# Last tokens of k and v in head halves, two v loads as bf16, and a new order of loads and of chunk 0's side work, in an attention and MLP kernel

## The chip, the core and the metric

The kernel runs on one core of one Trainium2 chip. The metric is the device time of one execution in microseconds; lower is better.

## The reference

```python
# q, k, v: (8 batches, 8 heads, 576 tokens, 64), fp32
q_s = exp(q - max(q)); q_s = q_s / sum(q_s, axis=-1)      # softmax over the head dimension
k_s = exp(k - max(k)); k_s = k_s / sum(k_s, axis=2)       # softmax over the tokens
kv  = einsum('bhsd,bhse->bhde', k_s, v)                   # one 64 x 64 matrix per head
x   = einsum('bhsd,bhde->bhse', q_s, kv)                  # then heads side by side: (8, 576, 512)
xn  = (x - mean(x)) / sqrt(var(x) + 1e-6) * g_ln
out = x + relu(xn @ w_ch1) @ w_ch2                        # w_ch1 512 x 2048, w_ch2 2048 x 512
```

## The kernel before

**Tiles and chunks.** A batch has 576 tokens: 512 main ones, token `4p + t` on partition `p` with `t` from 0 to 3, and 64 last ones. The program is a sequence of nine chunks of 512 tokens: chunks 0 to 7 are the main tokens of the batches, chunk 8 (`C9`) the last tokens of all eight batches together. For the keys, batch 0 has a layout of its own, 96 partitions of six tokens; in the others the key-value product of a pair of heads `j` (`kv_mm`, L239 to 263) takes four matmuls over the main tokens (`ek` as weights, `vm` as the moving operand, with a column of ones that gives the sum of k) and a fifth over the last tokens (`ekr`, `vr`). The last tokens of batch `b` lie on partitions 0 to 63 or 64 to 127, by the parity of `b`; the other half of `ekr` and `vr` is zero.

**A chunk.** The main stream of a chunk (`mlp_steps`) is its two MLP products: `mm1` (L406, 128x512 matmuls into `ph`, whose relu to `hT` is ACT's) or `mm1_part` (L421, the same on one or two of the four `t`), and then `mm2_stream` (L466) in chunk 0 and a seven-product scheme (L513, `ba` to `be`, with sums on DVE, L497) in the others. A chunk can start once its `xnT` is there: `x` from `po_mm` (L283) and `x_fast` (L329), normalized to `xn` on DVE, and transposed, either by the DMA (`xn_T`, on SP's queue) or by TensorE and a copy out of PSUM (`pe_T`, L788, called by `xn_pT` and `eq_pT`).

**The order** is written out by hand. `run` walks through the main stream, adds up a weight for every matmul (1 for 512 columns, 0.5 for 256), and emits each side step once the sum has reached the step's position. In chunk 0 positions run from 0 to 128. Each engine then works its instructions off in that order. Side steps of chunk 0 are the rest of batch 0's attention and all of batch 1's: exp of q, transposes of `eq`, exp of k, `cast_v` (L147, fp32 `vt` into bf16 `vm`, DVE), `prep_kvrem` (L155), `kv_all(1)` at 96, `po_x(1, t)` from 96.5 to 106, the transposes of `xn` at 104 to 126, and at 127 exp of q for batch 2. Chunk 1 holds batch 2's attention (`second_side`), chunk 2 batch 3's (`attn_fast`), and so on.

**Before chunk 0** stands `first_batch` (L812): batch 0's q (two of four `t`), k, exp, transposes, kv and po for `t` 0 and 1, with matmuls on zeros (`warm`) between them. Its DMAs: q and k on SP's queue, all others on POOL's, in this order: v (two blocks), w1 block 0, the other half of q, w1 blocks 1 to 3, w2 blocks 0 and 1. `load_behind(1)` (L911) then adds batch 1's q, k, v and last tokens, `load_w2` the last two blocks of w2, `load_behind(2)` batch 2's. A load on POOL's queue that writes another type than it reads is a cast in flight: the weights and batch 0's v come so. POOL's DMAs go round over eight semaphores, so that an issue waits for the landing of the one eight before it. Batches 3 to 7 are loaded on SP's queue, in the chunk two ahead.

The tile `vt` has one buffer, and batch 0's `ek` uses the same one; `kt` has one, `qt` two.

Of the kernel before, what the change touches and what calls it, by code (L numbers as in the profile page):

```python
# [12 lines left out]
FP32 = mybir.dt.float32  # L13
# [7 lines left out]
def kernel(  # L21
# [16 lines left out]
    nc = tc.nc  # L38
# [14 lines left out]
    C9 = B  # L53
    FAST = 1
    T0 = 6
    P0 = S // T0
# [25 lines left out]
    kv_sb = const.tile([P, B, NP, P], BF16)  # L82
    ekr = const.tile([P, 2, H, D], BF16)
    vr = const.tile([P, 2, NP, VW], BF16)
# [4 lines left out]

    def load_w1(nb):  # L90
        cols = slice(nb * 512, nb * 512 + 512)
        nc.gpsimd.dma_start(w1_sb[:, :, cols], w1_src[:, :, cols])
# [10 lines left out]
    def alloc_batch(b):  # L103
        raws[b] = (
            raw.tile([P, H, T, D], FP32, tag="kt", name="kt", bufs=1),
            raw.tile([P, H, T, D], FP32, tag="vt", name="vt", bufs=1),
            raw.tile([P, H, T, D], FP32, tag="qt", name="qt"),
            raw.tile([P, H, D], FP32, tag="ktr", name="ktr"),
            raw.tile([P, H, D], FP32, tag="vtr", name="vtr"),
        )  # L110
# [8 lines left out]
    def load_kvrem(eng, b):  # L119
        pb = SR * (b % 2)  # L120
        for src, dst in ((k, raws[b][3]), (v, raws[b][4])):
            eng.dma_start(dst[pb : pb + SR], src[b, :, SM:S, :].transpose([1, 0, 2]))

# [31 lines left out]
    def prep_kvrem(b):  # L155
        par = b % 2
        pb = SR * par
        nc.scalar.activation(ekr[pb : pb + SR, par], raws[b][3][pb : pb + SR], AF.Exp)
        nc.vector.tensor_copy(
            out=vr[pb : pb + SR, par, :, 0:P],  # L160
            in_=raws[b][4][pb : pb + SR].rearrange("p (j h) d -> p j (h d)", h=2),
        )

# [75 lines left out]
    def kv_mm(b, j, t):  # L239
        par = b % 2  # L240
        last = T if b else T0 - 1
        if j % 2 == 0 and t == 0:
            kvbox["p"] = att_ps.tile([P, 2, 256], FP32, tag="a", name="pkv")
        pkv = kvbox["p"]
        w = P + 1
        if b == 0:
            lhsT, rhs, w = k0_mm(j, t)
        elif t < T:
            lhsT, rhs = eks[b][:, t, 2 * j : 2 * j + 2, :], vm[:, par, t, j, 0 : P + 1]
        else:  # L250
            lhsT, rhs = ekr[:, par, 2 * j : 2 * j + 2, :], vr[:, par, j, 0 : P + 1]
        nc.tensor.matmul(  # L252
            pkv[:, j % 2, 0:w], lhsT, rhs, start=(t == 0), stop=(t == last)
        )
        if j % 2 == 1 and t == last:
            js = slice(j - 1, j + 1)
            rzk = recip_z(pkv[:, :, P]) if b else kvbox["rz", j // 2]
            for half in range(2):
                ps = slice(64 * half, 64 * half + 64)
                nc.vector.tensor_mul(  # L260
                    kv_sb[ps, b, js, ps], pkv[ps, :, ps],
                    rzk[ps].to_broadcast([64, 2, D]),
                )
# [51 lines left out]
    def square_sum(c, t):  # L315
        x, _, _, mv = xs[c]
        nc.scalar.activation(  # L317
            scrap, x[:, t], AF.Square, bias=mv[:, t, 0:1], accum_out=mv[:, t, 1:2]
        )
# [27 lines left out]
    def mean_x(c, t):  # L347
        nc.scalar.activation(
            scrap, pobox[c, t], AF.Copy, scale=-1.0 / DM, accum_out=xs[c][3][:, t, 0:1]
        )  # L350
# [289 lines left out]
    def mlp_steps(c):  # L640
        full = range(KO2)
        first, parts = [], ()
        if c == 0:
            full = range(0)
            parts = ((0, 0, 1), (0, 1, 1), (1, 0, 2), (2, 0, 2), (3, 0, 2), (0, 2, 2), (1, 2, 2), (2, 2, 2), (3, 2, 2))
        else:
            full, parts = range(4, KO2), ((0, 0, 2), (0, 2, 2))
        for n, t0, tn in parts:
            first += [
                (0.25 * tn, lambda m=m, t0=t0, tn=tn, ko=ko: mm1_part(c, m, t0, tn, ko))  # L650
                for m in range(4 * n, 4 * n + 4) for ko in range(KO1)
            ]
# [10 lines left out]
    def spread(fns, a, b):  # L663
        n = len(fns)
        return [(a + (b - a) * i / n, fn) for i, fn in enumerate(fns)]
# [63 lines left out]
    def sums_fast(c, t0=0):  # L729

        eq, zq, rq = eqs[c]
        s = spread([lambda t=t: nc.vector.reduce_sum(zq[:, t], eq[:, t], axis=AX.X) for t in range(T)][t0:], 0, 12)  # L732
        return s + [(12, lambda: nc.vector.reciprocal(rq, zq))]

# [14 lines left out]
    def second_side():  # L749

        s = [(p, lambda i=i: quarter_w2(i, 1)) for i, p in enumerate((1, 4, 44, 46))]
        s += [(42, lambda: square_sum(1, 2)), (46, lambda: square_sum(1, 3)), (54, lambda: rstd_op(1))]
        s += [(p, lambda w=w: load_batch(3, (w,))) for p, w in ((8, 2), (31, 0), (40, 1))]
        s += [(p + 11, fn) for p, fn in sums_fast(2)]
        s += [(12, lambda: exp_k(2, 0, 4)), (17, lambda: exp_k(2, 2, 4)), (23, lambda: prep_kvrem(2))]
        s += [
# [3 lines left out]
        s += spread(  # L760
            [lambda j=j, t=t: kv_mm(2, j, t) for j in range(NP) for t in range(T + 1)], 35, 48
        )
        s += [(49, lambda: start_x(2))]
        for t, (p0, p1) in enumerate(((51, 56), (66, 73), (76, 81), (87, 93))):
            s += spread([lambda t=t, i=i: po_mm(2, t, i) for i in range(NP)], p0, p1)
            s += [(p1, lambda t=t: x_fast(2, t)), ((63, 82, 92, 105)[t], lambda t=t: square_sum(2, t))]
        s += [(78, lambda: xn_T(2, 0, 2)), (98, lambda: xn_T(2, 2, 2)), (106, lambda: rstd_op(2))]
# [44 lines left out]
    def first_batch():  # L812
# [44 lines left out]
        nc.gpsimd.tensor_copy(out=gate[0:P0], in_=k0[0:P0, 5, 0, 0:4])  # L857
        load_w1(0)
        load_q0(1, nc.gpsimd)
        for nb in range(1, 4):  # L860
            load_w1(nb)
# [9 lines left out]
        exp_k0(0)  # L871
        nc.vector.memset(vr[:, :, :, P:], 1.0)
        nc.vector.memset(vr[:, :, :, 0:P], 0.0)
        nc.vector.memset(ekr, 0.0)
        nc.vector.memset(vm[:, :, :, :, P:], 1.0)
# [19 lines left out]
        xn, mv = xs[0][2], xs[0][3]  # L895
        stats(0, 0, pobox[0, 0], (slice(0, DH2), slice(DH2, DM)))
        mean_x(0, 1)
        warm(11)
        for i in range(2):
# [10 lines left out]

    def load_behind(b):  # L911

        alloc_batch(b)
        for which in (2, 0, 1):
            load_main(nc.gpsimd, b, which, 0, H)
        load_kvrem(nc.gpsimd, b)

# [11 lines left out]
    with tc.manual_schedule(  # L929
# [3 lines left out]
        first_batch()  # L933
        load_behind(1)
        load_w2(2)
        load_w2(3)
        load_behind(2)
# [5 lines left out]

        def kv_all(c):
            for j in range(NP):
                for t in range(T + 1):
                    kv_mm(c, j, t)
            start_x(c)

        run(  # L950
            mlp_steps(0),
            [
                (0.5, lambda: (xn_pT(0, 1, nc.scalar), exp_qt(0, 2), exp_qt(0, 3))),
                (8, lambda: (eq_pT(0, 2, nc.vector), eq_pT(0, 3, nc.vector))),
                (12, lambda: (q0_rest(2), x_fast(0, 2))),
                (14, lambda: (q0_rest(3), x_fast(0, 3))),
                (24, lambda: xn_pT(0, 2, nc.scalar)),
                (27, lambda: xn_pT(0, 3, nc.vector)),
                (28, lambda: square_sum(0, 2)),
                (32, lambda: square_sum(0, 3)),  # L960
                (34, lambda: (x_copy(0, 0), square_po(0, 1))),
# [5 lines left out]
            + [(67 + t, lambda t=t: reduce_q(1, t)) for t in range(T)]  # L967
            + [((72, 76, 86, 90)[t], lambda t=t: eq_pT(1, t, nc.scalar)) for t in range(T)]
            + [(78, lambda: nc.vector.reciprocal(eqs[1][2], eqs[1][1]))]
            + [(80, lambda: exp_k(1, 0, 4)), (84, lambda: exp_k(1, 2, 4))]  # L970
            + [(94 + 0.2 * j, lambda j=j: cast_v(1, j)) for j in range(NP)]
            + [(p, lambda i=i: quarter_w2(i, 0)) for i, p in enumerate((55, 58, 60, 62))]
            + [(95.9, lambda: prep_kvrem(1))]
            + [(96, lambda: kv_all(1))]
            + [(96.5, lambda: (po_x(1, 0), po_x(1, 1)))]
            + [(100, lambda: po_x(1, 2)), (104, lambda: xn_pT(1, 0, nc.scalar)), (105, lambda: square_sum(1, 0))]
            + [(106, lambda: po_x(1, 3)), (112, lambda: xn_pT(1, 1, nc.scalar)), (113, lambda: square_sum(1, 1))]
            + [(118, lambda: xn_pT(1, 2, nc.scalar))]
            + [(126, lambda: xn_pT(1, 3, nc.scalar)), (127, lambda: (exp_q(2, 0, 4), exp_q(2, 2, 4)))]
            + [(127.8, lambda: eq_T(2))],  # L980
        )
# [53 lines left out]
```

## Time and profile before

| | us |
|---|---|
| median of 5 runs (lowest, highest) | 284.0 (282.36, 285.41) |
| the profiled execution | 284.0 |
| its span (first to last instruction) | 282.2 |
| PE, DVE, ACT busy | 273.3, 196.6, 182.2 |
| first matmul of chunk 0, chunk 1, chunk 2 | 17.2, 54.5, 82.6 |
| HBM read and written | 36.7 MB, 9.4 MB |

A row of the page names line, engine, operation, output and inputs by the program's names, and after the bar busy time, the mean time of one in ns, and the engine's idle time before them with what ended most of it. `PEld` is the load of matmul weights. A line of the chain has start, length, and what the time went to; a line of a timeline has start, length, engine, line, operation, shape, count and, in brackets, the idle time before it and its releaser. A matmul's own length includes its way through the array; in a row of matmuls they start 216 (512 columns), 109 (256) or 56 ns (128) apart.

### The profile page before, as it was taken

The page shows a single profiled execution, that of the slowest core. Times are in us where ns is not written, and L with a number is a line of the kernel's source. Part 1 is how long each engine was busy: PE and PEld are TensorE (multiplying, and loading weights), DVE is VectorE, ACT ScalarE, POOL GpSimd, SP SyncE. Part 2 cuts the span into 40 slices and gives each one's busy share as a digit, 9 for nine tenths or more (in the row PEclk, how much of TensorE's full clock was granted, in tenths as well). Part 3 has the DMA queues.
Part 4 walks back from the last instruction along what each step waited for, and adds up shares of the span by engine and source line. Part 5 has one row for each costly group of instructions (what it writes and reads, how often), then busy time and mean ns, then how long its engine had stood idle before and what let it go on. Part 6 is the DMA issues. An engine that isn't in the chain of part 4 may idle for free.

```text
span 282.2 us, 5607 instructions
## 1 busy us (share of the span) xinstructions
PE 273.3 (97%) x2225; PEld 200.2 (71%) x2228; DVE 196.6 (70%) x452; ACT 182.2 (65%) x344; POOL 34.8 (12%) x61
## 2 busy tenths in 40 slices
PE   8989998999999999999999999999999999999994
PEld 6768855655996588649964986499659855885583
DVE  4655568967997778667866786678667939961363
ACT  4455882698786787597759775977586377526500
POOL 3653213300011002000110020002000200030000
PEclk9999999999999999999999999999999999999999
DMA  7999999999768985995399649953923420142014
GB/s 185 189 231 203 336 241 299 305 236 346 162 133 274 319 84 128 287 306 90 86 288 319 98 111 291 291 97 97 236 42 64 126 77 1 37 114 74 2 37 112
DMA packets 67084, 49.06 MB, mean 174 GB/s; under 512 B 40177, under 2 KB 63217, under 8 KB 67058
## 3 DMA queue, kind: packets, MB, share of 16 engines
q1 hardware_dynamic: 56914, 27.66, 42.4%
q0 software_dynamic: 9552, 20.52, 27.9%
q10 hardware_dynamic: 592, 0.52, 0.5%
q8 instruction: 17, 0.28, 0.4%
q14 instruction: 9, 0.07, 0.1%
HBM read 36.70 MB, written 9.44 MB: 163 GB/s over the span
## 4 chain that ended last, share of the span: by engine, by line
PE 73%; DMA 15%; DVE 7%; ACT 3%; issue 1%; POOL 0%; ACTq 0%; DVEq 0%
PE ph L406 25%; PE ba L513 17%; PE ph L421 9%; DMA vt<-in_v_dram 8%; DMA qt<-in_q_dram 4%; PE bb L513 4%; PE bc L513 4%; PE be L513 4%; PE pkv L252 2%; DMA v<-in_v_dram 2%; PE pc L466 2%; PE po L283 2%; ACT hT L394 2%; DVE hs L497 2%; DVE ot L524 1%
## 5 line engine op out<-in xcount | busy, mean ns | idle before, releaser
L406 PE MATMUL ph<-xnT,w_sb 128*128 128x512 bf16 x384 | 90.6, 379 | 0.0
L394 ACT ACTIVATE hT<-ph 128x512 bf16<-128x512 f32 x96 | 55.4, 597 | 17.4 <-PE ph L406 17.4
L406 PEld LDWEIGHTS <-w_sb 128*128 128x128 bf16 x384 | 35.6, 98 | 36.6
L513 PEld LDWEIGHTS <-hs 128*128 128x128 bf16 x512 | 49.1, 98 | 5.8 <-DVE hs L497 0.2
L421 PE MATMUL ph<-xnT,w_sb 128*128 128x256 bf16 (+1 forms) x400 | 49.3, 268 | 1.2 <-DMA w_sb<-in_moe_w_ch_dram 1.1
L431 ACT ACTIVATE hT<-ph 128x512 bf16<-128x512 f32 x44 | 25.8, 596 | 26.6 <-PE ph L421 26.6
L497 DVE TENSOR_TENSOR hs<-hT 128x1024 bf16<-128x1024 bf16 x32 | 21.9, 687 | 29.5 <-ACT hT L394 29.3
L513 PEld LDWEIGHTS <-hT 128*128 128x128 bf16 x384 | 36.6, 98 | 6.0 <-ACT hT L394 0.9
L421 PEld LDWEIGHTS <-w_sb 128*128 128x128 bf16 x400 | 35.1, 98 | 5.5 <-DMA w_sb<-in_moe_w_ch_dram 1.8
L530 POOL DMA_DIRECT2D out_dram<-ot x28 | 15.0, 540 | 182.6 <-DVE ot L524 182.6
L513 PE MATMUL ba<-w_q,hs 128*128 128x256 bf16 x256 | 31.3, 273 | 0.0
L323 DVE SCALAR_TENSOR_TENSOR xn<-x,mv,g_bc 128x512 bf16<-128x512 bf16 x34 | 25.5, 751 | 1.2
L330 DVE SCALAR_TENSOR_TENSOR x<-po,rq 128x512 bf16<-128x512 f32 x30 | 20.6, 685 | 7.1 <-PE po L283 6.8
L317 ACT ACTIVATE scrap<-x,mv 128x512 bf16<-128x512 bf16 x34 | 24.5, 720 | 0.4 <-DVE mv L336 0.2
L283 PE MATMUL po<-kv_sb,eqT 128*128 128x128 bf16 x128 | 24.0, 219 | 0.5 <-DVE kv_sb L260 0.5
L252 PE MATMUL pkv<-vm,ek 128*128 128x129 bf16 x112 | 21.8, 220 | 0.0
L538 ACT COPY s<-ba 128x512 f32<-128x512 f32 x15 | 8.8, 586 | 15.9 <-PE ba L513 15.6
L283 PEld LDWEIGHTS <-eqT 128*128 128x128 bf16 x128 | 11.5, 98 | 7.7 <-issue 0.9
L513 PE MATMUL ba<-w_sb,hT 128*128 128x256 bf16 x128 | 16.4, 273 | 0.5 <-ACT hT L394 0.5
L732 DVE TENSOR_REDUCE zq<-eq 128x8 f32<-128x512 bf16 x26 | 16.3, 692 | 0.1
L176 ACT ACTIVATE eq<-qt 128x1024 bf16<-128x1024 f32 x14 | 14.5, 1054 | 2.1 <-DMA qt<-in_q_dram 2.1
L513 PE MATMUL bb<-w_q,hs 128*128 128x256 bf16 x128 | 15.7, 273 | 0.0
(121 smaller groups left out, 343.6 us busy)
## 6 DMA issues: line engine op xcount, KB each, us to landing
out_dram<-ot POOLq DMA_DIRECT2D x32, 256.0 KB, 2.9
qt<-in_q_dram SPq DMA_DIRECT2D x5, 1024.0 KB, 7.0
kt<-in_k_dram SPq DMA_DIRECT2D x5, 1024.0 KB, 9.8
vt<-in_v_dram SPq DMA_DIRECT2D x5, 1024.0 KB, 12.6
w_sb<-in_moe_w_ch_dram POOLq DMA_DIRECT2D x8, 512.0 KB, 14.1
qt<-in_q_dram POOLq DMA_DIRECT2D x2, 1024.0 KB, 19.0
kt<-in_k_dram POOLq DMA_DIRECT2D x2, 1024.0 KB, 16.5
vt<-in_v_dram POOLq DMA_DIRECT2D x2, 1024.0 KB, 18.0
```

The costliest lines, as they stand in the source:

```text
L252: nc.tensor.matmul(pkv[:, j % 2, 0:w], lhsT, rhs, start=(t == 0), stop=(t == last))
L283: nc.tensor.matmul(pobox["p"][:, i * P : i * P + P], eqTs[c][:, t, i, :], kv_sb[:, c, i, :], start=True, stop=True,)
L317: nc.scalar.activation(scrap, x[:, t], AF.Square, bias=mv[:, t, 0:1], accum_out=mv[:, t, 1:2])
L323: nc.vector.scalar_tensor_tensor(xn[:, t], in0=x[:, t], scalar=mv[:, t, 0:1], in1=g_bc, op0=ALU.add, op1=ALU.mult)
L330: nc.vector.scalar_tensor_tensor(x[:, t].rearrange("p (h d) -> p h d", h=H), in0=pobox[c, t].rearrange("p (h d) -> p h d", h=H), scalar=1. ...
L394: nc.scalar.activation(dst, src, AF.Relu)
L406: nc.tensor.matmul(hbox["ph"], w1_sb[:, ko, m * P : (m + 1) * P], xnTs[c][:, :, ko, :], start=(ko == 0), stop=(ko == KO1 - 1),)
L421: nc.tensor.matmul(ph[:, m % 2, at : at + tn], w1_sb[:, ko, m * P : (m + 1) * P], xnTs[c][:, t0 : t0 + tn, ko, :], start=(ko == 0), stop=( ...
L431: nc.scalar.activation(dst, ph, AF.Relu)
L497: nc.vector.tensor_tensor(out=dst, in0=x, in1=y, op=op)
L513: nc.tensor.matmul(hbox[bank][:, t], lhsT, rhs, start=first and (own or t == 0) and k == 0, stop=k == KH - 1, skip_group_check=True)
L732: s = spread([lambda t=t: nc.vector.reduce_sum(zq[:, t], eq[:, t], axis=AX.X) for t in range(T)][t0:], 0, 12)
```

## The change

- The last tokens of k and v go by halves of the heads: heads 0 to 3 on partitions 0 to 63, heads 4 to 7 on 64 to 127, for every batch. Two DMAs become four, `ekr` is half as wide, exp works on 128 x 256 instead of 64 x 512, the copy into `vr` becomes two of 64 x 256. The number and shape of kv matmuls stay.
- `vt` of batches 1 and 2 is bf16; their loads, on POOL's queue, cast in flight, and `cast_v` copies bf16.
- POOL's queue: the other half of batch 0's q comes ahead of w1 block 0, which comes in two halves of 256 columns; w2 block 2 comes ahead of batch 1's v.
- `first_batch` takes exp of that q half and the transposes of `eq` for `t` = 2 in among its own work; two `warm` matmuls fewer.
- Chunk 0: the quarter `(3, 0, 2)` of its first product goes later; the rest of batch 0's attention moves earlier, batch 1's from `cast_v` on later; the kv products of the last tokens stand 1.5 positions behind the others (and use both PSUM tiles). Exp and transposes of q for batch 2, and the fourth transpose of `xn` for batch 1, move into chunk 1.
- Chunk 1: two blocks of its first product instead of one are done by halves of `t`, both first halves first; batch 2's attention is placed later in it.

```diff
+    CAST = (1, 2)
...
-    ekr = const.tile([P, 2, H, D], BF16)
+    ekr = const.tile([P, 2, H // 2, D], BF16)
...
+    def load_w1(nb, c0=0, c1=512):
+        cols = slice(nb * 512 + c0, nb * 512 + c1)
...
-            raw.tile([P, H, T, D], FP32, tag="vt", name="vt", bufs=1),
+            raw.tile([P, H, T, D], BF16 if b in CAST else FP32, tag="vt", name="vt", bufs=1),
...
     def load_kvrem(eng, b):
-        pb = SR * (b % 2)
         for src, dst in ((k, raws[b][3]), (v, raws[b][4])):
-            eng.dma_start(dst[pb : pb + SR], src[b, :, SM:S, :].transpose([1, 0, 2]))
+            for half in range(2):
+                eng.dma_start(
+                    dst[SR * half : SR * half + SR],
+                    src[b, 4 * half : 4 * half + 4, SM:S, :].transpose([1, 0, 2]),
+                )
...
     def prep_kvrem(b):
...
+        nc.scalar.activation(ekr[:, par], raws[b][3], AF.Exp)
+        for half in range(2):
+            ps = slice(SR * half, SR * half + SR)
+            nc.vector.tensor_copy(
+                out=vr[ps, par, 2 * half : 2 * half + 2, 0:P],
+                in_=raws[b][4][ps].rearrange("p (j h) d -> p j (h d)", h=2),
+            )
...
-            parts = ((0, 0, 1), (0, 1, 1), (1, 0, 2), (2, 0, 2), (3, 0, 2), (0, 2, 2), (1, 2, 2), (2, 2, 2), (3, 2, 2))
+            parts = ((0, 0, 1), (0, 1, 1), (1, 0, 2), (2, 0, 2), (0, 2, 2), (1, 2, 2), (2, 2, 2), (3, 0, 2), (3, 2, 2))
...
+            if c == 1:
+                full, parts = range(8, KO2), ((0, 0, 2), (1, 0, 2), (0, 2, 2), (1, 2, 2))
...
     def second_side():
...
+        s += [(8.0, lambda: xn_pT(1, 3, nc.scalar))]
+        s += [(10, lambda: exp_q(2, 0, 4)), (14, lambda: exp_q(2, 2, 4)), (14.2, lambda: eq_T(2))]
...
-            [lambda j=j, t=t: kv_mm(2, j, t) for j in range(NP) for t in range(T + 1)], 35, 48
-        )
-        s += [(49, lambda: start_x(2))]
-        for t, (p0, p1) in enumerate(((51, 56), (66, 73), (76, 81), (87, 93))):
+            [lambda j=j, t=t: kv_mm(2, j, t) for j in range(NP) for t in range(T + 1)], 43, 53
+        )
+        s += [(53, lambda: start_x(2))]
+        for t, (p0, p1) in enumerate(((55, 58), (64, 67), (75, 80), (87, 93))):
...
-        load_w1(0)
         load_q0(1, nc.gpsimd)
+        load_w1(0, 0, 256)
+        load_w1(0, 256, 512)
...
+        exp_qt(0, 2)
         mean_x(0, 1)
-        warm(11)
+        exp_qt(0, 3)
+        warm(6)
+        eq_pT(0, 2, nc.scalar)
+        warm(3)
...
-        load_behind(1)
+        load_behind(1, (2, 0))
         load_w2(2)
+        load_behind(1, (1,))
         load_w2(3)
         load_behind(2)
...
-                (0.5, lambda: (xn_pT(0, 1, nc.scalar), exp_qt(0, 2), exp_qt(0, 3))),
-                (8, lambda: (eq_pT(0, 2, nc.vector), eq_pT(0, 3, nc.vector))),
-                (12, lambda: (q0_rest(2), x_fast(0, 2))),
-                (14, lambda: (q0_rest(3), x_fast(0, 3))),
-                (24, lambda: xn_pT(0, 2, nc.scalar)),
-                (27, lambda: xn_pT(0, 3, nc.vector)),
+                (0.5, lambda: xn_pT(0, 1, nc.scalar)),
+                (1.5, lambda: (q0_rest(2), x_fast(0, 2))),
+                (3, lambda: eq_pT(0, 3, nc.scalar)),
+                (6, lambda: (q0_rest(3), x_fast(0, 3))),
+                (9, lambda: xn_pT(0, 2, nc.scalar)),
+                (15, lambda: xn_pT(0, 3, nc.scalar)),
...
-            + [(94 + 0.2 * j, lambda j=j: cast_v(1, j)) for j in range(NP)]
+            + [(98.5 + 0.2 * j, lambda j=j: cast_v(1, j)) for j in range(NP)]
...
-            + [(95.9, lambda: prep_kvrem(1))]
-            + [(96, lambda: kv_all(1))]
-            + [(96.5, lambda: (po_x(1, 0), po_x(1, 1)))]
-            + [(100, lambda: po_x(1, 2)), (104, lambda: xn_pT(1, 0, nc.scalar)), (105, lambda: square_sum(1, 0))]
-            + [(106, lambda: po_x(1, 3)), (112, lambda: xn_pT(1, 1, nc.scalar)), (113, lambda: square_sum(1, 1))]
-            + [(118, lambda: xn_pT(1, 2, nc.scalar))]
-            + [(126, lambda: xn_pT(1, 3, nc.scalar)), (127, lambda: (exp_q(2, 0, 4), exp_q(2, 2, 4)))]
-            + [(127.8, lambda: eq_T(2))],
+            + [(100.4, lambda: prep_kvrem(1))]
+            + [(100.5, lambda: kv_main(1)), (102.0, lambda: kv_rest(1))]
+            + [(108.0, lambda: po_x(1, 0)), (110.0, lambda: po_x(1, 1))]
+            + [(113.0, lambda: po_x(1, 2)), (114.9, lambda: xn_pT(1, 0, nc.scalar)), (115.9, lambda: square_sum(1, 0))]
+            + [(115.9, lambda: po_x(1, 3)), (121.0, lambda: xn_pT(1, 1, nc.scalar)), (122.0, lambda: square_sum(1, 1))]
+            + [(128.0, lambda: xn_pT(1, 2, nc.scalar))]
```

## The prediction

> **What bounds the kernel now.** I read the page first, then the chain of waits in order of time, then PE's timeline, then the DMA issues one by one.
>
> ```profile
> PE 273.3 (97%) x2225; PEld 200.2 (71%) x2228; DVE 196.6 (70%) x452; ACT 182.2 (65%) x344; POOL 34.8 (12%) x61
> ...
> DMA  7999999999768985995399649953923420142014
> ```
>
> TensorE is busy all along, yet the DMA engines (one digit is 7.06 us) are full for the first ten slices. Which of the two sets the end of the opening is told by the chain:
>
> ```profile
> 19.32 22.54 DMA vt<-in_v_dram
> 41.88 1.48 DVE vm L153 x4
> 43.39 0.44 DVE vr L159
> 43.87 0.51 PE pkv L252 x6
> ...
> 54.69 3.49 PE ph L421 x32
> ```
>
> Until 41.9 us the chain is one transfer, batch 1's v (v1 below; k1, q1 alike); then four casts, the copy of its last tokens, the key-value products (kv), and from 54.7 on TensorE to the end. From chunk 3 on each chunk takes 28.1 us, and 32 matmuls of 109 ns, 48 of 216, 112 of 109 and 36 of 56 add to 28.1: nothing is to be had there. Chunk 2 takes 0.6 more, a hole at 99.0 behind ACT's exp of q, whose load (85.6 to 93.7) and place stay; I leave it as it is. So what counts is when the last kv product of batch 1 runs, and how much of TensorE's program is still queued behind it. PE's timeline of the opening has the holes:
>
> ```profile
> 21.10 1.05 PE L421 MATMUL ph<-xnT,w_sb 128*128 128x256 bf16 x8 [0.72 <-DMA w_sb<-in_moe_w_ch_dram]
> ...
> 26.22 0.83 PE L421 MATMUL ph<-xnT,w_sb 128*128 128x256 bf16 x6 [0.38 <-DMA w_sb<-in_moe_w_ch_dram]
> ...
> 43.87 0.22 PE L252 MATMUL pkv<-vr,ekr 128*128 128x129 bf16 x1 [0.45 <-DVE vr L159]
> ...
> 46.08 0.49 PE L283 MATMUL po<-kv_sb,eqT 128*128 128x128 bf16 x6 [0.53 <-DVE kv_sb L260]
> ...
> 54.52 1.69 PE L421 MATMUL ph<-xnT,w_sb 128*128 128x256 bf16 x14
> ```
>
> Counted from start to start against 216, 109 and 56 ns, 2.9 us are lost between 14.95 and 43.03 us (weights late), 1.7 us around kv.
>
> **The queue.** Times from issue to landing of single loads on POOL's queue (KB, us):
>
> ```profile
> kt<-in_k_dram POOLq DMA_DIRECT2D x1, 1024.0 KB, 20.7
> vt<-in_v_dram POOLq DMA_DIRECT2D x1, 1024.0 KB, 22.5
> ktr<-in_k_dram POOLq DMA_DIRECT2D x1, 128.0 KB, 21.1
> vtr<-in_v_dram POOLq DMA_DIRECT2D x1, 128.0 KB, 19.2
> w_sb<-in_moe_w_ch_dram POOLq DMA_DIRECT2D x1, 512.0 KB, 18.6
> ```
>
> Issued at 16.6, 19.3, 21.3, 23.9 and 26.5, they land at 37.3, 41.8, 42.4, 43.1 and 45.0. The whole list: second v of batch 0 13.1, w1 block 0 16.3, q0b (batch 0's other q half) 18.8, w1 blocks 1 to 3 at 21.1, 23.7, 26.2, w2 blocks 0 and 1 at 28.7 and 31.2, q1 34.3, k1 37.3, v1 41.8, and as above. Hence the prices: 2.5 us for a weight block, 3.0 us for 1 MB in fp32, and 45.0 - 37.3 - 3.0 - 2.5 = 2.2 us for k's and v's last tokens together. In plain first-in order v1 would land at 40.3 and vtr at 42.5; they came 1.5 and 0.6 later, since neighbours overlap.
>
> **The change, part by part.**
>
> 1. *w1 block 0 in two halves, behind q0b.* The order leaves the sum alone. The halves make pieces of 512 B where the block had 1 KB: a block's 512 pieces take 2.5 us (4.9 ns each), batch 0's v, 384 pieces of 768 B, 1.42 us (3.7 ns). Between 2.5 us (by bytes) and 3.05 (both pieces' packet times extended) I take 2.8: **+0.3**. q0b lands at 13.1 + 0.76 (the first load's start) + 2.43 = 16.25. TensorE now has the transposes of eq(0,2) between its warm-ups: exp of 0.62 us puts them at 16.9, 1.4 after the first six warm-ups; ACT then works off mean_x, exp_qt(0,3) and a copy before the two xnT copies, so the first ph is at about 18.8 instead of 17.2. Free only under cover of the queue, see 5.
>
> 2. *w2 block 2 ahead of v1.* **+2.5** for v1 and its last tokens; the 0.29 us that PE waited for this block at 45.06 go.
>
> 3. *v1 as bf16.* 1024 pieces of 512 B: the same 2.8 instead of 3.0, **-0.2**. The cast becomes a bf16 copy, which no row shows from SBUF. Ends: 0.35 us from start to start (the fp32 rows, 1.48 for four) and half of it; I take 0.25, so the fourth is done 1.05 us after the first starts. Batch 2's v, which landed at 57.1 and was cast from 60.7, has cover.
>
> 4. *Last tokens by head halves.* Bytes and pieces stay; two DMAs become four, alternating between the partition halves. The Trainium skill (DMA: Bandwidth & Descriptors, Rules for kernel authors) says of two transfers to disjoint partition halves "Don't bother": they serialize on the same 16 engines. By it the 2.2 us stay. The row against it: the eight qr loads of batch 6's stage, 128 KB each and alternating halves, on SP's queue; the third lands at 203.2 and the eighth at 205.6, 0.47 us each, where ktr and vtr on POOL's cost 1.1. Ends 0.9 and 2.2; I take **1.5**. The POOL queue holds eight loads: each issue waits for the landing of the one eight before. v1's waits for w1 block 1 (21.4), the four halves' for later weights (24 to 31.5): all long before their turn. On ACT exp is 256 elements wide (an estimate of 0.41, from 0.63 at 512 and 1.05 at 1024), on DVE two copies of about 0.29 replace 0.42.
>
> Sum: k1 lands at 37.6, w2 block 2 at 40.1, v1 at 42.9 plus a lag of 0.9 (less than before's 1.5, the neighbours being shorter) = 43.8, the last half of vtr at 42.9 + 1.5 + 0.6 = 45.0. Casts end at 44.9, the second vr copy starts then or when its half has landed, after the first copy: 45.5. **Last kv product at 45.55**, against 44.72 before: 0.85 later.
>
> 5. *The new chunk 0 order.* It must let TensorE be there in time. Before, 25.2 us of work lay between 14.95 and 43.03; now five mm2 matmuls more and two warm-ups fewer, 26.1, plus 2.7 of waits from part 1: at the kv products at 43.7, where the first cast is ready at 44.1. Against the last kv product the slack is half a microsecond.
> Behind the kv products chunk 0 has left, by the built order, 26 mm2 matmuls (5.62), 16 po and 12 transposes (1.57) and 0.1 of waits: 7.3, chunk 1 at 52.85. Before there were 32, 16 and 16 and 1.1 of waits: 9.8, at 54.52. So chunk 1 starts **1.65 us earlier**. The price: the fourth xn transpose stands in chunk 1 (0.22), and 64 half-width matmuls there instead of 32 and 16 wide ones (0.04 more). Net -1.4.
>
> 6. *Moved into chunk 1.* xn_pT(1,3) stands at step 8, 16 matmuls after the chunk's first, 55.0; its xn is the fourth of a DVE chain of 1.58 us each from 47.2, so 53.6. exp_q(2) and exp_k(2) stand among relus on ACT (16 of 0.5 us and 4 of 1.05 in 14 us): covered. eq_T(2) now stands behind batch 3's q on SP: issued at about 57.5, it shares the engines with that 1 MB (3.0), batch 2's tail and chunk 0's stores, and lands at 63 to 65.5; po(2,0) at step 55 needs it at 66. Cover about 1 us, and beyond it PE stalls in order. The five SP batches behind have four small loads for two; SP ends them at 95.2 in chunk 2, the transposes behind it wait for xn until 97.0 and are needed at 111.5.
>
> The profiled execution took 284.0 us (span 282.2), which is also the median of the runs shown: 284.0 - 1.4 = **282.6**.
>
> **Rivals.** (a) *The forecast*, 0.50; its own range 281.6 to 283.8.
> (b) *A cast costs by the piece.* Every cast load in the trace has one packet per piece, where fp32 loads pack four; if a 512 B piece costs a w1 piece's 4.9 ns, w1's halves and v1 take 5.0 us each, 2.2 more than I take, and the last kv product is at 49.95: 282.6 + 4.4 = **287.0**. It decides (slower than before) once the queue is over 1.4 us later than forecast. Against it stands batch 0's v, at 3.7. Chance 0.12.
> (c) *The queue is quicker and TensorE binds.* If q0b, whose 128 packets of 4 KB the trace could move in 1.6 us, lands near 15, part 1's waits shrink by 1.2; with last tokens at 0.9 and no lag, kv's end is set by TensorE's arrival, 42.5 + 1.1 = 43.6: **280.7**. Chance 0.22.
> (d) *The change does not do what it says*: halves serialize, 2.2 us, copies stay at 0.35. vtr at 45.7, last kv at 46.3: **283.3**. Chance 0.16.
>
> A rule on the clock bears on (a): the skill (TensorE: Matmul & The Clock Gate, its table for kernels) warns of PE-idle gaps over about 3 us, after which the clock is halved for 3.4 us. Part 1's 1.4 and 1.1 lie apart by 0.9 of work; the holes of before (up to 0.9) left the granted clock at full. By the rule at its worst 1.7 us of work would be lost, of which 0.5 are covered: 283.8, inside the range.
>
> **Numbers.** Range 280.4 to 285.2: below it lies the best of (c), above it most of (b). Over 1% (2.8 us, about what a measurement of this kernel can tell): faster (c) and the edge of (a), 0.27; slower (b) and a late eqT, 0.14; within, 0.59.
>
> **What would show it.** In the profile after: v1 landing at 43 to 44.5; the last pkv<-vr,ekr near 45.5; the first 256-wide ph of chunk 1 near 52.9, no hole of 0.53 for kv_sb; first ph later than before; chunks from 3 on at 28.1. The forecast is wrong if v1 lands after 45.5 or before 42.5, if kv waits neither for vm nor vr, if po(2,0) waits for eqT, or if PEclk drops near 17.

## The result, and the profile after

The changed kernel takes **281.2 us** (median; 280.4 to 283.4) against 283.1 us for the kernel before in runs on the same chip: ratio 0.9929, 95% interval 0.9911 to 0.9948. That is 1.9 us less (1.5 to 2.5 by the interval), where 1.4 us was forecast and 282.6 us predicted. The profiled execution of the changed kernel took 280.9 us (span 279.2).

The page of the changed kernel: busy time of the engines, and the DMA engines' share in 40 slices.

```profile
PE 272.8 (98%) x2239; PEld 201.7 (72%) x2242; DVE 194.9 (70%) x456; ACT 182.0 (65%) x347; POOL 37.7 (14%) x66
...
DMA  6999999999949945994599469944914410141014
```

The sums hardly move. The DMA engines are full for the first eleven slices, as they were for ten before; what changed is which of the two sides the chain of waits follows in the opening (start, length, what):

```profile
12.63 10.86 DMA w_sb<-in_moe_w_ch_dram
23.54 10.65 PE ph L427 x96
...
52.08 1.75 PE ph L427 x16
```

Before, the chain lay on the transfer of v1 until 41.9 us. Now the last transfer on it is w1 block 2, landed at 23.49, and from 23.54 us on it is TensorE, but for DVE's work on kv and x (44.3 to 48.6). So the queue has stopped being the bound around the key-value products (kv), as rival (c) had it. TensorE's timeline there:

```profile
42.91 1.07 PE L257 MATMUL pkv<-vm,ek 128*128 128x129 bf16 x16
...
44.03 0.40 PE L257 MATMUL pkv<-vr,ekr 128*128 128x129 bf16 x4
...
46.02 0.27 PE L289 MATMUL po<-kv_sb,eqT 128*128 128x128 bf16 x2 [0.18 <-DVE kv_sb L266]
...
48.66 0.38 PE L289 MATMUL po<-kv_sb,eqT 128*128 128x128 bf16 x4 [0.19 <-DVE x L336]
...
51.92 1.91 PE L427 MATMUL ph<-xnT,w_sb 128*128 128x256 bf16 x16
```

Neither kv group has a bracket: no wait for `vm` or `vr`. The last kv product starts at 44.03 + 3 x 0.056 = 44.2 us (44.7 before), and chunk 1's first 256-wide `ph` at 51.92 (54.52 before): 2.6 us earlier. The landings behind it, from the DMA issues on POOL's queue (KB, us from issue to landing; w2 block 2 is issued at 18.65, batch 1's v at 21.52, the last of the four halves, of v, at 31.43, w2 block 3 at 34.40):

```profile
w_sb<-in_moe_w_ch_dram POOLq DMA_DIRECT2D x1, 512.0 KB, 20.7
...
vt<-in_v_dram POOLq DMA_DIRECT2D x1, 512.0 KB, 20.8
...
vtr<-in_v_dram POOLq DMA_DIRECT2D x1, 64.0 KB, 11.7
...
w_sb<-in_moe_w_ch_dram POOLq DMA_DIRECT2D x1, 512.0 KB, 11.1
```

v1 lands at 42.27 and all last tokens at 43.13, 0.86 us behind it. All in all, from the landing of the load ahead of v1 to that of the load behind the last tokens (w2 block 2 at 39.31, w2 block 3 at 45.46) 6.15 us pass. In the kernel before the same stretch (k1 at 37.27, w2 block 2 at 45.02) took 7.75. This stretch, called **block to block** below, is the measure used for the queue, because neighbouring loads overlap and single landings mislead. It drifts too: in the three other profiles with these loads in this order (improved, q_first, q0b_behind) it is 5.9 to 6.4 us, and the last tokens land 0.8 to 1.4 us behind v1.

The two profiles differ by 3.0 us of span: chunk 1 starts 2.6 us earlier, and chunk 2's hole of 0.6 us at 99.0 is missing in this execution, against about 0.26 of work moved into chunk 1. The timed medians differ by 1.9 only: before's profiled execution lay 0.9 us above its median of 283.1, after's 0.3 below its own.

### The profile page after: what moved, and what is told of

Its sections match the earlier page's. It is cut to its first block, busy times and chain, and to the rows that moved or that the text cites. A ratio compares the mean times of both kernels' runs of the same rounds, so it can differ in the third digit from the quotient of the medians.

```text
span 279.2 us, 5663 instructions
## 1 busy us (share of the span) xinstructions
PE 272.8 (98%) x2239; PEld 201.7 (72%) x2242; DVE 194.9 (70%) x456; ACT 182.0 (65%) x347; POOL 37.7 (14%) x66
## 4 chain that ended last, share of the span: by engine, by line
PE 89%; DMA 6%; DVE 2%; POOL 1%; SPq 1%; issue 0%; POOLq 0%
PE ph L412 28%; PE ba L519 20%; PE ph L427 15%; PE bb L519 5%; PE bc L519 5%; PE be L519 5%; DMA w_sb<-in_moe_w_ch_dram 4%; PE pc L472 4%; PE pkv L257 3%; DMA kt<-in_k_dram 2%; PE po L289 2%; POOL w_sb L93 1%; PE po L296 1%; PE ptr L800 1%; DVE x L336 0%; DVE kv_sb L266 0%
## 5 line engine op out<-in xcount | busy, mean ns | idle before, releaser
L412 PE MATMUL ph<-xnT,w_sb 128*128 128x512 bf16 x368 | 87.2, 379 | 0.0
L412 PEld LDWEIGHTS <-w_sb 128*128 128x128 bf16 x368 | 34.0, 98 | 34.5 <-issue 0.2
L427 PE MATMUL ph<-xnT,w_sb 128*128 128x256 bf16 (+1 forms) x432 | 53.1, 269 | 0.3 <-DMA w_sb<-in_moe_w_ch_dram 0.2
L427 PEld LDWEIGHTS <-w_sb 128*128 128x128 bf16 x432 | 38.4, 98 | 4.6 <-DMA w_sb<-in_moe_w_ch_dram 0.7
L197 DVE TENSOR_REDUCE zq<-eq 128x8 f32<-128x512 bf16 x32 | 20.2, 690 | 4.2 <-ACT eq L189 2.2
L257 PE MATMUL pkv<-vm,ek 128*128 128x129 bf16 x112 | 21.2, 220 | 0.0
## 6 DMA issues: line engine op xcount, KB each, us to landing
kt<-in_k_dram SPq DMA_DIRECT2D x5, 1024.0 KB, 10.3
```

The costliest lines, as they stand in the source:

```text
L197: nc.vector.reduce_sum(eqs[c][1][:, t], eqs[c][0][:, t], axis=AX.X)
L257: nc.tensor.matmul(pkv[:, j % 2, 0:w], lhsT, rhs, start=(t == 0 and j % 2 == 0), stop=(t == last), skip_group_check=True,)
L412: nc.tensor.matmul(hbox["ph"], w1_sb[:, ko, m * P : (m + 1) * P], xnTs[c][:, :, ko, :], start=(ko == 0), stop=(ko == KO1 - 1),)
L427: nc.tensor.matmul(ph[:, m % 2, at : at + tn], w1_sb[:, ko, m * P : (m + 1) * P], xnTs[c][:, t0 : t0 + tn, ko, :], start=(ko == 0), stop=( ...
```

## Experiments

"Above" and "under" in us are differences of the ratios to the kernel before, times 283.

### The last tokens: the old layout, smaller loads, opposite halves

**one_load** puts the old layout of the last tokens back into the changed kernel.

```diff
-            for half in range(2):
-                eng.dma_start(
-                    dst[SR * half : SR * half + SR],
-                    src[b, 4 * half : 4 * half + 4, SM:S, :].transpose([1, 0, 2]),
-                )
+            eng.dma_start(dst[pb : pb + SR], src[b, :, SM:S, :].transpose([1, 0, 2]))
```

> The changed kernel, but k's and v's last tokens in the old way: all 8 heads on one half of the partitions, one load each, one copy. Theory 1 (the halves freed the queue: k1's to the last token's landing costs 0.85 us behind v1 instead of some 2, so that TensorE and not the queue sets the key-value products): the last token of v lands at 44.1 to 44.6 instead of 43.13, TensorE stands before pkv<-vr,ekr for 0.8 to 1.2 us, and the time is 0.8 to 1.2 us above the changed kernel's. Theory 2 (only the new order of chunk 0 and of the loads counts): no wait there, the time of the changed kernel.

Ratio 0.9989 (0.9970 to 1.0008), 1.7 us above the changed kernel: nearly the whole gain is gone. v's landing, the last tokens' and w2 block 3's (issued at 21.55, 26.32 and 28.86), and TensorE's wait, in one_load:

```profile
vt<-in_v_dram POOLq DMA_DIRECT2D x1, 512.0 KB, 21.6
w_sb<-in_moe_w_ch_dram POOLq DMA_DIRECT2D x1, 512.0 KB, 18.2
...
vtr<-in_v_dram POOLq DMA_DIRECT2D x1, 128.0 KB, 19.0
```

```profile
45.80 0.40 PE L253 MATMUL pkv<-vr,ekr 128*128 128x129 bf16 x4 [1.01 <-DVE vr L160]
...
68.52 0.23 PE L285 MATMUL po<-kv_sb,eqT 128*128 128x128 bf16 x1 [1.34 <-DMA eqT<-eq]
```

v and the last tokens land at 43.14 and 45.30, 2.16 us apart (0.86 in the changed kernel); block to block 7.70 (39.40 to 47.10) against 6.15. The kv products come 1.8 us later and so does chunk 1 (53.70). The second row is another wait, taken up below.

**split_same** keeps one_load's layout but cuts each load by heads into two that go to the same 64 partitions.

```diff
-            eng.dma_start(dst[pb : pb + SR], src[b, :, SM:S, :].transpose([1, 0, 2]))
+            for half in range(2):
+                hs = slice(4 * half, 4 * half + 4)
+                eng.dma_start(dst[pb : pb + SR, hs], src[b, hs, SM:S, :].transpose([1, 0, 2]))
```

> As one_load, but each last-token load is cut by heads into two of 64 KB that go to the SAME 64 partitions. Theory 1a (what makes the last tokens quick is that both partition halves are written): 2 us for the four, as one_load, and its time. Theory 1b (smaller loads are quick by themselves, whatever the partitions): the four land within 0.9 us behind v1, and the time is within 0.3 us of the changed kernel's.

Neither: 0.9964 (0.9944 to 0.9985), 1.0 us above. The four land within 1.47 us behind v1; block to block 6.72. The copy into `vr` also took longer here (0.76 against 0.42 us for the same shape in one_load), and TensorE waited for it. Cutting the loads also delays the issue of w2 block 3 behind them (34.1 us instead of 28.9, since four loads take four of the eight semaphores); no run separates that from the smaller size.

```profile
44.84 0.40 PE L257 MATMUL pkv<-vr,ekr 128*128 128x129 bf16 x4 [0.72 <-DVE vr L164]
```

**opposite** leaves one_load's two loads of 128 KB but sends v's to the other half of the partitions.

```diff
             eng.dma_start(dst[pb : pb + SR], src[b, :, SM:S, :].transpose([1, 0, 2]))
+            pb = SR - pb
```

> one_load with v's last tokens on the other half of the partitions than k's: still two loads of 128 KB, now one to each half. (The last tokens' share of the key-value product of batches 1 to 7 is thereby left out of the sum; the instructions and their sizes stay.) Measured so far from v1's landing to vtr's: 2.16 us for two loads on one half, 1.47 for four on one half, 0.86 for four in turn on both halves. Theory 1a (the partition halves make it quick): 1.1 to 1.4 us here, pkv<-vr,ekr waits 0.2 to 0.4 us, and the time is 0.5 to 1 us below one_load's. Theory 1b (only the size of the loads does): 2.1 us and one_load's time.

0.9971 (0.9947 to 0.9995), 0.5 us under one_load by the medians, with overlapping intervals; what the halves do is read from the queue. v (issued at 20.63) lands at 42.89 and the last tokens, issued at 25.40, at 43.89, 1.00 us later; w2 block 3, issued at 28.02, at 46.12:

```profile
vt<-in_v_dram POOLq DMA_DIRECT2D x1, 512.0 KB, 22.3
w_sb<-in_moe_w_ch_dram POOLq DMA_DIRECT2D x1, 512.0 KB, 18.1
...
vtr<-in_v_dram POOLq DMA_DIRECT2D x1, 128.0 KB, 18.5
```

Block to block is 6.79, and `pkv<-vr,ekr` waits no more (`pkv<-vm` does, 0.91 us for v). So each half of the edit brings about 0.95 us on the queue in these profiles (7.70 to 6.72 by more and smaller loads on one half, 7.70 to 6.79 by the two halves alone), and both together 1.55. The split between the two is loose: one_load_low, below, has one_load's layout and took 7.04. The last tokens' lag behind v (2.16 and 2.08 us in those two, 1.00 here) separates the layouts better. The Trainium skill (DMA: Bandwidth & Descriptors, Rules for kernel authors) advises against splitting over disjoint partition halves, since they serialize. In this place two loads of unchanged size gained 0.3 to 0.9 us, by the two profiles of the old layout, from the halves alone.

**one_load_low** exchanges the halves of odd and even batches, to see whether the upper half is the slow one.

```diff
-        pb = SR * (b % 2)
+        pb = SR * ((b + 1) % 2)
```

> one_load with the partition halves of odd and even batches exchanged: batch 1's last tokens go to the lower 64 partitions and batch 2's to the upper. In one_load, batch 1's (upper half, w2 block 3 queued behind them) took 2.16 us from v1's landing and 7.7 us from w2 block 2's landing to w2 block 3's; batch 2's (lower half, no load queued behind) 0.74. Theory A (the load behind them on the queue, not the half, makes the old layout slow): as one_load, 7.4 to 8.0 us between the two w2 blocks and about 0.75 for batch 2; the time of one_load. Theory B (the upper half is the slow one): 6.0 to 6.5 us between the w2 blocks and the time of the changed kernel, batch 2 over 1.5 us.

v1 to last tokens 2.08 us, block to block 7.04, which lies between what the two theories expected, and 0.68 for batch 2, which now lies on the upper half. Its time, 0.9954 (0.9924 to 0.9984), lies between the changed kernel and one_load, and its interval overlaps both. Theory B does not fit: the slow batch stays slow on the lower half (2.08) and the quick one quick on the upper (0.68). What batch 1's loads have and batch 2's lack is a weight block directly behind them on the queue. In batch 2 the old layout costs nothing: from k2's landing to the last tokens' 3.23 us pass in one_load and 3.23 in the changed kernel. No run moves that weight block alone, so that it makes the difference is argued, not shown, and why it should stays open.

### The cast of v

**v_fp32** loads v of batches 1 and 2 as fp32 again.

```diff
-    CAST = (1, 2)
+    CAST = ()
```

> The changed kernel with v of batches 1 and 2 loaded as fp32 again and cast by DVE. Theory 1: v1 lands 0.3 to 0.5 us later, the four casts take 1.5 instead of 0.9 us, the last kv product is 0.6 to 0.9 us later, and the time 0.6 to 0.9 us above the changed kernel's. Theory 2: no difference, TensorE arrives later than either.

0.9973 (0.9954 to 0.9991), 1.2 us above, more than expected. The casts and TensorE's wait for the first of them, in v_fp32's timelines:

```profile
43.14 1.43 DVE L157 CAST vm<-vt 128x512 bf16<-128x512 f32 x4 [3.99 <-DMA vt<-in_v_dram]
```

```profile
43.62 1.40 PE L257 MATMUL pkv<-vm,ek 128*128 128x129 bf16 x16 [0.43 <-DVE vm L157]
```

The changed kernel's four copies take 0.90 us from 42.30. From w2 block 2 to v1 it is 3.66 us instead of 2.96, and block to block 6.90 instead of 6.15: the cast in flight saves 0.7 us of queue, not 0.2 (0.55 to 0.96 against the four profiles with these loads and the cast). Chunk 1 starts at 52.96, 1.0 later.

### Loads alone, order alone

**loads_only** is the kernel before with the cast and the halves, and its old order of loads and program. **order_only** is the complement: the new orders, v as fp32 and the last tokens in one load each.

On the kernel before (loads_only; `prep_kvrem`, `kv_mm` and `ekr` follow as in the change):

```diff
-            raw.tile([P, H, T, D], FP32, tag="vt", name="vt", bufs=1),
+            raw.tile([P, H, T, D], BF16 if b in (1, 2) else FP32, tag="vt", name="vt", bufs=1),
...
-            eng.dma_start(dst[pb : pb + SR], src[b, :, SM:S, :].transpose([1, 0, 2]))
+            for half in range(2):
+                eng.dma_start(
+                    dst[SR * half : SR * half + SR],
+                    src[b, 4 * half : 4 * half + 4, SM:S, :].transpose([1, 0, 2]),
+                )
```

On the changed kernel order_only is the edits of one_load and v_fp32 together.

> The kernel before with v of batches 1 and 2 as bf16 and the last tokens by halves, but its old order of loads and program. Theory 1 (TensorE reaches the key-value products at 43.0 whatever the queue does, so of the 2 us that the queue gains only the waits of before's 44 us stretch can go): v1 lands near 40.5, the waits of 0.45 for vr and 0.29 for w2 block 2 go, chunk 1 starts 0.7 to 1.1 us earlier than before's 54.5, time 0.6 to 1.1 us under before. Rival (the queue's gain comes through whole): 2 us under before.

0.9971 (0.9947 to 0.9996): 0.8 us under the kernel before. v1 lands at 38.89, 3.0 us earlier than before, of which 1.1 us was there already at k1. The kv products have no wait left, and TensorE loses 0.54 us on `kv_sb` right behind them as before the change. Chunk 1 starts at 52.93, more than expected, since this execution's q0b landed 1.2 us earlier than in before's profile and TensorE reached the kv products at 42.04 instead of 43.03; 1.5 us were lost again in chunk 2.

> The changed kernel's order of the program and of the loads, with v as fp32 and the last tokens in one load each as before the change. Theory 1 (the order brings nothing as long as the queue is late): v1's fp32 load (+0.9 by v_fp32) and the last tokens (+1.3 by one_load) put vtr at 46.0 to 46.5, pkv<-vr,ekr at 47, chunk 1 at 54.4 to 55: the time of the kernel before, or up to 1.5 us more if po(2,0) then waits for eqT as in one_load. Theory 2 (the order is what counts): within 0.5 us of the changed kernel.

0.9991 (0.9959 to 1.0022), the time of the kernel before, as theory 1 had it. v1 lands at 43.59, the last tokens at 45.14, block to block 8.10. Chunk 1 starts at 53.53, earlier than theory 1 had it and 1.0 us earlier than before; this execution lost it again in chunk 2, whose hole was 1.5 us instead of 0.6, and in the moved work. TensorE waited 0.71 us for `vm`, although the granted clock of this execution stood at 0.5 from 14.1 to 17.5 us and made TensorE late itself. By the medians the two parts bring 0.8 and 0.3 us, and together 2.0. The intervals are 0.7 and 0.9 us wide to a side, so that the sum isn't ruled out. That the order leaves TensorE waiting for a slower queue is shown by the waits in one_load, v_fp32 and here; how much the order is worth without the faster queue stays open.

### How close the queue is: w2_ahead and w2_behind

**w2_ahead** loads w2 block 3 ahead of v1 too.

```diff
-        load_behind(1, (1,))
         load_w2(3)
+        load_behind(1, (1,))
```

> The changed kernel with w2 block 3 also ahead of batch 1's v: v1 and its last tokens land 2.5 us later. It measures the queue's slack against TensorE. Theory 1 (TensorE binds, but the queue is only some 0.4 us ahead of it): the key-value products wait 2.0 to 2.3 us and the time is as much above the changed kernel's. Theory 2 (the queue is far ahead): less than 1 us. If the queue itself were still the bound: the full 2.5 us.

1.0066 (1.0042 to 1.0089): 3.9 us above, more than any of the three cases. v1 lands 2.2 us later, the kv products start 1.9 us later. TensorE's timeline, and the granted clock of the same stretches (start:end, length, busy times and counts of PE, PEld, DVE, ACT and POOL, granted clock, DMA share, GB/s):

```profile
44.85 1.41 PE L257 MATMUL pkv<-vm,ek 128*128 128x129 bf16 x16 [2.81 <-DVE vm L157]
```

```profile
46.80:48.80 2.00, 2.00 (x8) 0.87 (x7) 1.50 (x6) 0.00 (x0) 2.00 (x4) 0.50 1.04 352
48.80:52.00 3.20, 3.20 (x29) 1.79 (x27) 2.31 (x7) 0.24 (x1) 0.24 (x1) 1.00 1.24 254
```

The idle 2.81 us cost more than themselves: the clock then stands at 0.50, from 45.4 to 48.8 us, and from kv to chunk 1 the kernel needs 10.3 instead of 9.0 us. Chunk 1 starts 3.3 us later, and po(2,0) waited another 2.1 us for eqT in this execution. The timed runs show the clock's part: the mean granted clock of this execution is 0.994, and the fourteen runs at 0.992 to 0.994 have a median of 285.9 us, the eight at 0.997 and above one of 284.2, 3.0 us above the changed kernel. That v1 came 2.2 us later and the kv products 1.9 puts the queue's slack at 0.3 us.

**w2_behind** puts w2 block 2 behind v1 again.

```diff
-        load_behind(1, (2, 0))
+        load_behind(1)
         load_w2(2)
-        load_behind(1, (1,))
```

> The changed kernel with w2 block 2 behind batch 1's v and last tokens again: v1 lands near 39.7, the last tokens near 40.6, w2 block 2 near 43. Theory 1 (TensorE, not the queue, sets the key-value products in the changed kernel): nothing is gained by 2.5 us of earlier v, and mm2, which needs w2 block 2 from 42.0 on, waits about 1 us for it: 0.5 to 1.2 us above the changed kernel. If the queue were the bound: up to 2 us under it.

0.9956 (0.9933 to 0.9979), 0.8 us above. v1 lands at 39.85, the copies of v are done by 40.8, those into `vr` by 41.8, and nobody takes them: TensorE stands for the weights instead.

```profile
43.14 1.24 PE L472 MATMUL pc<-w_sb,hT 128*128 128x512 bf16 x5 [0.85 <-DMA w_sb<-in_moe_w_ch_dram]
```

So an earlier v is worth nothing in the changed kernel, and moving w2 block 2 forward is worth about 0.8 us by itself: the intervals overlap, but the wait is in the trace.

### q0b ahead of w1

**q0b_behind** loads the two halves of w1 block 0 first.

```diff
-        load_q0(1, nc.gpsimd)
         load_w1(0, 0, 256)
         load_w1(0, 256, 512)
+        load_q0(1, nc.gpsimd)
```

> The changed kernel with q0b behind the two halves of w1 block 0 instead of ahead of them. Theory (the new order of chunk 0 needs q0b first: the transposes of eq(0,2) stand in TensorE's program ahead of the first ph): q0b lands near 18.4 instead of 14.8, the first ph comes near 20 instead of 17.5, of this 0.6 us is given back by weight blocks 1 and 2, for which nobody waits any more: 1.8 to 2.4 us above the changed kernel. Rival (the first ph waits for its own weights anyway): under 0.5 us.

1.0108 (1.0078 to 1.0138), 5.1 us above: the direction was right, the size twice as large. q0b lands at 19.35, and the transposes of eq(0,2) hold all behind them in TensorE's program:

```profile
20.06 0.61 PE L800 MATMUL ptr<-ident,eq 128*128 128x128 bf16 x4 [4.51 <-ACT eq L189]
```

The first `ph` comes at 21.98 instead of 17.49, and again the granted clock falls to 0.50, here from 19.4 us, still in the idle stretch, to 26.2. The first and the last of four stretches (columns as above):

```profile
20.00:22.00 2.00, 1.69 (x12) 1.35 (x13) 0.75 (x1) 2.00 (x7) 0.40 (x1) 0.50 1.24 206
...
25.00:28.00 3.00, 3.00 (x41) 2.90 (x39) 2.06 (x6) 2.07 (x4) 0.79 (x2) 0.80 1.24 206
```

All six runs have a mean granted clock of 0.987 to 0.991. The lead of q0b is a condition of the new order; no run gives it to the old one.

### A version with three places moved

**improved** changes three positions in the changed kernel: batch 1's po two matmuls later, batch 3's q load behind the transpose of eq(2) on SP, and chunk 2's first exp of q later on ACT.

```diff
-            + [(108.0, lambda: po_x(1, 0)), (110.0, lambda: po_x(1, 1))]
+            + [(110.0, lambda: po_x(1, 0)), (112.0, lambda: po_x(1, 1))]
...
-        s += [(p, lambda w=w: load_batch(3, (w,))) for p, w in ((8, 2), (31, 0), (40, 1))]
+        s += [(p, lambda w=w: load_batch(3, (w,))) for p, w in ((14.4, 2), (31, 0), (40, 1))]
...
-        s = [(34, lambda: exp_q(b, 0, 4)), (73, lambda: exp_q(b, 2, 4)), (77, lambda: eq_T(b))]
+        s = [(48 if b == 4 else 34, lambda: exp_q(b, 0, 4)), (73, lambda: exp_q(b, 2, 4)), (77, lambda: eq_T(b))]
```

> The changed kernel with three places moved: po of batch 1 two mm2 matmuls later (its waits of 0.35 us for kv_sb and 0.35 for po's buffer at 45.6 and 48.3), batch 3's q load behind the transpose of eq(2) on SP instead of ahead of it (eqT landed at 65.2 in the changed kernel, and 1.5 to 2.1 us too late in one_load, split_same and w2_ahead), and chunk 2's first exp of q 14 steps later on ACT (a hole of 0 to 1.5 us near 98 in seven of the profiles). Theory (these waits come and go between executions and are part of the median): 0.5 to 1.2 us under the changed kernel, and no wait at these three places. Rival (they are hidden by something else on TensorE's path, or new ones take their place): within 0.3 us.

0.9909 (0.9880 to 0.9937), 0.6 us under the changed kernel by the ratios; the two intervals overlap, so that it clearly beats the kernel before, and the changed one only by its profile and its spread (280.5 to 281.4 in six runs). Its span is 278.7 us. The landing of eqT, in the changed kernel and then in improved:

```profile
eqT<-eq SPq DMA_TRANSPOSE x1, 7.8
```

```profile
eqT<-eq SPq DMA_TRANSPOSE x1, 4.6
```

It lands at 61.3 where it is needed at 64.7. In the timeline of improved the waits at kv_sb and at po's buffer are gone, and chunk 1 starts 0.6 us earlier:

```profile
45.58 0.39 PE L289 MATMUL po<-kv_sb,eqT 128*128 128x128 bf16 x4
...
51.29 1.91 PE L427 MATMUL ph<-xnT,w_sb 128*128 128x256 bf16 x16
```

**q_first** takes back one of the three moves, the q load's.

```diff
-        s += [(p, lambda w=w: load_batch(3, (w,))) for p, w in ((14.4, 2), (31, 0), (40, 1))]
+        s += [(p, lambda w=w: load_batch(3, (w,))) for p, w in ((8, 2), (31, 0), (40, 1))]
```

> The improved kernel with batch 3's q load ahead of the transpose of eq(2) on SP again, as in the changed kernel; the other two moves stay. Theory (that load makes the transpose's landing drift between 65 and 68 us from execution to execution, and po(2,0) needs it at about 65.5): eqT lands 3 to 6 us later than improved's 61.3, po(2,0) waits up to 2 us in a part of the executions, the median is 0.3 to 1 us above improved's and the spread of the runs two or three times as wide. Rival (the transpose is hidden): improved's median within 0.2 us and its spread.

0.9913 (0.9886 to 0.9939), the median of improved: on the median the expectation missed. The spread is as expected wider: eight of its ten runs lie at 280.3 to 280.8 us, two at 281.9 and 282.0. In the profile eqT landed at 65.08, 0.13 us late. A late eqT is an event of some executions, which a median does not show. But it need not be what makes these two runs long: the one at 281.9 has a mean granted clock of 0.994, as w2_ahead's profile with its stretch at half clock has. The changed kernel's runs look alike: 22 of 28 at 280.4 to 282.0, six at 282.5 to 283.4, of which two (282.8 each) have a clock of 0.994 and 0.993; which of the others waited for eqT was not profiled.

## Why the prediction was right, and where its steps were not

The time came out 1.4 us under the forecast, inside its range and between the forecast and rival (c). **The mechanism was rival (c)'s**: TensorE arrives, and nothing waits. Two of the signs that the prediction named for a wrong forecast are there: v1 lands before 42.5 (42.27), and kv waits neither for `vm` nor for `vr`. The sum for the last kv product failed (45.55 forecast, 44.2 measured), by terms of the queue. That 1.9 us came out near the 1.4 forecast is in part luck: the two profiles differ by 3.0.

1. *w1's halves and q0b.* The forecast put q0b at 16.25 and the first `ph` at 18.8; they came at 14.81 and 17.49. The step that failed is q0b's interval of 0.76 + 2.43 us behind batch 0's v, the second part taken from its old place, where it landed behind a weight block; in front it landed 1.42 us behind v, and the expected waits of 1.4 and 1.1 us did not come. In the ten other profiles with q0b in front it landed at 14.3 to 15.2, 1.4 to 3.0 us behind v, and waits came in part, 0.4 to 1.5 us together. The +0.3 for smaller pieces does not show: from batch 0's v to the end of q0b and w1 block 0 it is 4.97 us, against 5.69 before, and 4.69 in loads_only with the old pieces and order; the drift between executions is larger than the term.
2. *w2 block 2 ahead of v1* was sized right: 2.32 us on the queue for 2.5, and the wait for it gone. w2_behind shows that without it TensorE would wait 0.85 us, not 0.29, since it now gets there sooner.
3. *v as bf16*: -0.2 forecast, 0.7 measured by v_fp32. Rival (b), a cast charged by the piece, is refuted for v, with the opposite sign. The copies' interval, 0.25 estimated, was 0.2.
4. *Last tokens by halves*: 1.5 us chosen between 0.9 and 2.2; measured 0.86, and 0.8 to 1.6 in the seven other profiles with the halves. By blocks the forecast's terms make 2.8 + 1.5 + 2.5 = 6.8 us, against 6.15. The row of batch 6's qr loads was the nearer neighbour. That the two halves "serialize", rival (d), was wrong here. The lag of v1 (0.9) was too long as well: w2 block 2 to v1 was 2.96 us in all.
5. *Chunk 0's order* was the core of the forecast and holds: 7.3 us behind the last kv product forecast, 7.7 measured from 44.2 to 51.92. The difference is 0.35 us lost for kv_sb and 0.14 for po's buffer, where 0.1 was allowed. (Before the `po` at 48.66 the trace leaves 0.36 us from start to start, but there a second-product matmul lacks its record: its weight load stands at 48.25, and one_load's and v_fp32's traces show it in this place.) TensorE arrived at 42.9, not at 43.7, because step 1's waits were missing.
6. *eqT(2)* was given a landing at 63 to 65.5 and a cover of 1 us. It landed at 65.19 in the profile, and po(2,0) took it at 65.24: no cover at all, since chunk 1 had started a microsecond sooner than forecast. In five of the ten other profiles with the new chunk 1 and the q load ahead of it, it came 1.4 to 2.1 us late. This term was understated; it costs the change a part of its gain in some executions.

The clock's downside did not occur in the changed kernel's profile (granted clock 1.0), because the idle stretch it rested on did not; two of its 28 runs, at 0.994 and 0.993, may have met it. The runs bear out the rule, from the Trainium skill (TensorE: Matmul & The Clock Gate, its table for kernels), in w2_ahead and q0b_behind, where the clock was halved after idle stretches of 2.81 and 4.51 us. It does not account for order_only, whose clock was halved from 14.1 us on behind an idle 0.72 us.

**Chunk 2's hole** was left in the forecast as fixed, and is not. It goes with how long batch 4's q load is under way on SP: in the twelve profiles with exp of q in its old place 8.1 to 9.7 us went with a hole (0.3 to 1.5 us), 7.0 to 7.6 with none. In improved and q_first, whose exp of q comes later, loads of 8.4 and 8.7 us left none. It comes and goes in variants whose first two chunks differ in all ways; the 0.6 us between the two profiles are no effect of the change that a run here shows.

## What to carry to other kernels

When two limits lie within a microsecond, price each of them to that precision and then ask which is later: here the slower queue of one_load and v_fp32 cost the reordered program 1.8 and 1.0 us up to chunk 1, and once TensorE was the later of the two an earlier v was worth nothing. Measure a load in a full queue from the landing ahead of it to the landing behind it, and a small load by the row that resembles it in placement, not by its old row. A term that one profile shows as a hole or as a cover may be an event of that execution: look at it in several profiles before it enters the sum.

## What the runs showed of the hardware that was not expected

- The last tokens of k and v (256 KB in 256 B pieces) with a weight block queued behind, v as bf16, took from block to block 7.0 to 7.7 us as two loads on one partition half (one_load_low, one_load), 6.8 as two loads on opposite halves (opposite), 6.7 as four on one half (split_same), and 5.7 to 6.4 as four on both (six profiles). With no load queued behind, in batch 2, they took 0.7 to 1.1 us behind v in every layout of the changed kernel, but 1.7 in the kernel before, where a DMA transpose on SP's queue ran at the same time.
- TensorE idle for 2.81 us (w2_ahead) was followed by 3.4 us at half the granted clock; 14 of its 22 runs have a mean clock of 0.994 or less. Idle for 4.51 us (q0b_behind), the clock was halved for 6.8 us, and all six runs show it. 1.3 us of idle time (one_load) did not halve it, yet 3.4 us at half clock followed an idle 0.72 us in order_only, where the stretch before held small matmuls; why stays open.
- The same DMA transpose of eq(2) took 4.6 to 6.5 us from issue to landing ahead of a 1 MB load on SP's queue (improved, the kernel before, loads_only), and 7.4 to 10 us behind one.
